# Due times that count each engine's load, and output products that stand behind two units

## The chip, the cores and the metric

The kernel runs on one core of a Trainium2 chip. Its time is the device time of one execution in microseconds; the kernel before takes 1060.63 us (median of 3 runs, 1060.13 to 1060.71). The engines are called as in the profile: PE (matmuls; PEld is its weight load), DVE, ACT and POOL (elementwise engines), and SP, whose queue issues nearly all DMAs.

## The reference

Attention with random features on 8 batches x 8 heads x 576 tokens x 64, and then a gated product on all 4608 tokens:

```python
def phi(x):
    proj = np.einsum('bhsd,md->bhsm', x, omega)
    h = proj - np.sum(x * x, axis=-1, keepdims=True) / 2.0
    h = h - np.max(h, axis=-1, keepdims=True)
    return np.exp(h) / np.sqrt(m)
q_p, k_p = phi(q_s), phi(k_s)
kv = np.einsum('bhsm,bhsd->bhmd', k_p, v);  z = np.sum(k_p, axis=2)
num = np.einsum('bhsm,bhmd->bhsd', q_p, kv)
den = np.einsum('bhsm,bhm->bhs', q_p, z)[..., None] + 1e-06
x = (num / den) ...          # 4608 tokens x 512
a = x @ w_a;  b = x @ w_b    # 512 x 1536 each
return a * b @ w_out         # 1536 x 512
```

## The kernel before

**Numbers.** The second part needs more precision than one pass of PE gives, so each operand is split into a high and a low half and a product is three matmuls (high by high, high by low, low by high).

**Blocks.** The gated product runs in blocks of 512 tokens, b = 0 to 8 (the ninth holds the 64 last tokens of each batch). For b = 0 and 1 (`moe_block`) a step computes `pa` (12 matmuls of 512 columns), `pb` (12), and the four output products `o` of an earlier step (12). From b = 2 on (`moe_block7`) two steps of 128 columns and 512 tokens are computed as a two by two block product with seven instead of eight products. One such run is a **unit** (`unit`): seven products of six matmuls of 256 columns, called A to G here in the order in which they are issued, on two PSUM tiles: A on `p0`, B and C on `p1`, D and E on `p0`, F and G on `p1`. DVE adds (L1253) take them into the sum tile `c`. The add behind C reads both halves of `p1`, and F overwrites a half of it, so F waits for that add. Two units (w = 0 and 1) make one index i; their sums are multiplied (L1303) and split into `ghl` (L333 or L335, and L341), which is what the output products read.

**Output products.** They are collected in the list `left` and issued by `flush` between the products of later units, with a priority number near those units'. For b = 7 and 8 they are a seven product form as well (L1032).

**Attention.** While block b runs on PE, the attention of the next batch is computed pair of heads by pair of heads: `four` (L512: features of keys and queries into the two PSUM tiles `at`), exponentials on ACT, `pkv` (L754), the product `pm` (L822) with rows that went through DRAM, and copies on ACT that free `at` again: `x` from `pm`, `xts` and `k2` from `pkv` (L333). The next `four` needs both `at` tiles, so it waits for the copy `k2`. DVE divides (L773 to L779), ACT scales by it (L783).

**What sets the order.** Nothing of this is issued in the order in which it is written. Each operation is recorded with its engine and an estimated duration, and `plan` then makes a schedule: `schedule` takes, again and again, the operation that can start first on its engine. Where several could start at about the same time, a number decides: on PE and SP the priority `prio`, on DVE, ACT and POOL the due time `due`. Due times come from `dues`, which walks back from the PE's times in the last schedule. `plan` schedules once without due times and three times with them (`ROUNDS`) and keeps the order whose last operation ends first. Each engine then runs its instructions strictly in that order, with semaphores for the dependences.

Of the kernel before, what the change touches and what calls it, by code (L numbers as in the profile page):

```python
# [1 line left out]

# [16 lines left out]
B, H, S, D, M = 8, 8, 576, 64, 128  # L19
# [16 lines left out]
EPS = 1e-6 * M  # L36
KS = NHP

CFG = dict(PORT=0.5, EDF=("DVE", "ACT", "POOL"), ROUNDS=3, SQUEEZE=1, ZS=800, ZB=(1500, 3000, 5000), ZD=(1500, 3000, 4500), HQ=(2500, 4000, 5000), BACK2=(1500, 2500, 4000), TW=(), WAIT=150, RAW=2000, FAST=(0, 1, 2, 3), JOIN0=False, WARM=8, HROOM=["w0", "u1", "w1", "u2", "w2", "u3"], H=3, TURN=(7,), BACK=1500, AT=2, GATES=(-4, -1, 2, 5), SQPE=4, MARGIN=1200, LOAD=2500, SUMS=1000, NATS=(1, 2, 3), CONV=(28000, 2600))

# [14 lines left out]
class Graph:  # L57
# [78 lines left out]
    def dues(self):  # L136

        inf = 1e12
        after = {o: [(n, o) for n in ()] for o in self.ops}
        for o in self.ops:  # L140
            for d in o.deps:
                after[d].append(o)

        last = {}
        for o in self.order:
            for b in o.alloc:
                if b.slot in last:
                    for x in last[b.slot].users:
                        if x is not o:
                            after[x].append(o)  # L150
                last[b.slot] = b
        idle, at, ideal = 0, 0, {}
        for o in self.order:
            if "PE" in o.eng:
                idle += max(0, o.start - at - 5) * CFG["SQUEEZE"]
                at = o.end
                ideal[o] = o.start - idle
        for o in reversed(self.order):
            d = ideal[o] + o.eng["PE"] if o in ideal else inf
            for n in after[o]:  # L160
                same = "PE" in o.eng and "PE" in n.eng
                cost = n.end - n.start if n.bytes else next(iter(n.eng.values()))
                d = min(d, n.due - cost - n.margin - (0 if same else self.LAT + (150 if "PE" in o.eng else 0)))
            o.due = d

    def plan(self):

        self.schedule()
        plans = [(max(o.end for o in self.order), 0, None)]
        for k in range(CFG["ROUNDS"]):  # L170
            self.dues()
# [3 lines left out]
        _, k, due = min(plans, key=lambda p: p[:2])  # L175
        if k < CFG["ROUNDS"]:
            for o in self.ops:
# [4 lines left out]
    def schedule(self, bw=330.0, dma_lat=2000):  # L182
# [29 lines left out]
        while len(done) < len(self.ops):  # L212
            best = None
            for e in engines:
                mine = None
                for o in ready[e]:
# [7 lines left out]
                    else:  # L224


                        wait = CFG["WAIT"] if e == "DVE" and 0 <= o.prio < 4000 else 0
                        pr = o.prio if o.due is None or e not in CFG["EDF"] else o.due
                        key = (max(s - wait, free[e] + 30), pr, o.n)
# [15 lines left out]
            else:  # L245
                o.end = s + o.eng[e]
                if e == "DVE" and o.port:
                    o.end += CFG["PORT"] * max(0, min(o.end, free["POOL"]) - s)
                free[e] = max(s + 30, o.end - self.OVER[e])
# [43 lines left out]
def tile_attention_moe(ctx: ExitStack, tc: tile.TileContext, kqt, kqtt, kqn, kqnt, vx, omst, idn, wab, wout, out):  # L293
    nc = tc.nc
    SQPE = CFG["SQPE"]
# [104 lines left out]
    late = [f"{r}{k}" for k in range(NF - 1, -1, -1) for r in "uw"]  # L400
# [525 lines left out]
    MOE = 10 ** 6  # L926
# [3 lines left out]
    left = []  # L930
# [233 lines left out]

    def flush(seq, n=99):
        for _ in range(min(n, len(left))):
            left.pop(0)(MOE + seq)

# [37 lines left out]
    def moe_block7(b):  # L1208
# [10 lines left out]
        def unit(i, w, C):  # L1219
# [43 lines left out]

            k = 0 if i == NFP - 1 and w else 1
            flush(seq + 3, 5 if i == w == 0 else k)
            product(p0, 1, tcol(tA, 1), (tA, None), scol(0), sr[0], 4)
            if ones7 and w == 0:
# [4 lines left out]

            add(slice(3, 4), p0, slice(1, 2), lambda: c4.ap[:, 1:2], [1], [3])
            flush(seq + 6, k)
            product(p1, 0, tcol(tB, 1), (tB, None), xcol(2, hi_half), xr(2), 7)
            product(p1, 1, lambda k, c: bq.ap[:, k, P * c:P * c + P], (bq, None), scol(3), sr[1], 8)
# [170 lines left out]
```

## Time and profile before

| what | value |
|---|---|
| median of 3 runs | 1060.63 us |
| profiled execution, first to last instruction (span) | 1057.4 us |
| PE busy | 1042.8 us, 7806 matmuls |
| PE weight load busy | 919.1 us |
| DVE busy | 885.7 us |
| ACT busy | 594.5 us |
| POOL busy | 106.0 us |
| granted clock of PE, mean | 0.998 |
| DMA | 314.16 MB, mean 297 GB/s |

The profiled execution is known by its span; the median of the runs is 1060.63 - 1057.4 = 3.2 us more, which is what lies around the first and the last instruction. PE is busy nearly all the time, so its idle stretches and its slow stretches are what an order can change. PE's busy time is modelled from overlapping matmuls; the starts of consecutive matmuls tell more than the sum. A timeline row has the start (us), the length from the first start to the last end, the engine, the line, the names, and in square brackets the idle time before it with what ended it.

### The profile page before, as it was taken

The page shows a single profiled execution, that of the slowest core. Times are in us where ns is not written, and L with a number is a line of the kernel's source. Part 1 is how long each engine was busy: PE and PEld are TensorE (multiplying, and loading weights), DVE is VectorE, ACT ScalarE, POOL GpSimd, SP SyncE. Part 2 cuts the span into 40 slices and gives each one's busy share as a digit, 9 for nine tenths or more (in the row PEclk, how much of TensorE's full clock was granted, in tenths as well). Part 3 has the DMA queues.
Part 4 walks back from the last instruction along what each step waited for, and adds up shares of the span by engine and source line. Part 5 has one row for each costly group of instructions (what it writes and reads, how often), then busy time and mean ns, then how long its engine had stood idle before and what let it go on. Part 6 is the DMA issues. An engine that isn't in the chain of part 4 may idle for free.

```text
span 1057.4 us, 22019 instructions
## 1 busy us (share of the span) xinstructions
PE 1042.8 (99%) x7806; PEld 919.1 (87%) x7806; DVE 885.7 (84%) x2226; ACT 594.5 (56%) x1642; POOL 106.0 (10%) x177
## 2 busy tenths in 40 slices
PE   9999999999999999999999999999999999999998
PEld 7877777877788888888989898989898988999998
DVE  6999999899998688879787788878776677998767
ACT  7897788678765475656455565565464123232211
POOL 0121111111111010201011111111010000000000
PEclk9999999999999999999999999999999999999999
DMA  9777797999899889988989888989888899999991
GB/s 357 274 248 248 239 308 248 315 332 330 280 301 384 279 283 342 312 308 285 326 309 328 295 311 299 341 277 303 270 262 282 274 304 310 325 325 337 354 326 52
DMA packets 123646, 314.16 MB, mean 297 GB/s; under 512 B 17680, under 2 KB 40976, under 8 KB 123536
## 3 DMA queue, kind: packets, MB, share of 16 engines
q1 hardware_dynamic: 122656, 312.10, 86.4%
q8 instruction: 61, 1.00, 0.4%
q10 hardware_dynamic: 880, 0.66, 0.2%
q14 instruction: 49, 0.40, 0.1%
HBM read 255.52 MB, written 57.18 MB: 296 GB/s over the span
## 4 chain that ended last, share of the span: by engine, by line
PE 86%; DVE 8%; ACT 2%; DMA 2%; issue 1%; SPq 0%; DVEq 0%; ACTq 0%
PE p L1243 39%; PE o L962 19%; PE ppk L512 5%; PE o_P L1032 5%; PE pa L1151 4%; PE pb L1151 4%; PE pkv L754 2%; PE pm L822 2%; DVE raw L387 1%; DVE sm L535 1%; PE pn L896 1%; PE p L1032 1%; PE ppq L512 1%; DVE c L1253 1%; PE pkv L884 1%
## 5 line engine op out<-in xcount | busy, mean ns | idle before, releaser
L1253 DVE TENSOR_TENSOR c<-p,c 128x512 f32<-128x512 f32 (+1 forms) x336 | 207.5, 618 | 83.2 <-PE p L1243 79.4
L962 PE MATMUL o<-wo,ghl 128*128 128x512 f32 x1008 | 270.1, 397 | 0.0
L962 PEld LDWEIGHTS o<-wo,ghl 128*128 128x128 f32 x1008 | 176.1, 188 | 31.2 <-DVE ghl L341 0.2
L1243 PE MATMUL p<-Sa,t 128*128 128x256 f32 x1008 | 143.1, 281 | 0.0
L1243 PEld LDWEIGHTS p<-Sa,t 128*128 128x128 f32 x1008 | 131.6, 188 | 4.5
L707 POOL TENSOR_TENSOR z<-hk 128x256 f32<-128x256 f32 x56 | 45.0, 804 | 668.8 <-ACT hk L548 530.9
L783 ACT ACTIVATE hq<-hq,dn 128x128 f32<-128x128 f32 x224 | 70.3, 393 | 33.1 <-DVE dn L779 28.7
L333 ACT COPY c<-p 128x256 f32<-128x256 f32 x84 | 31.1, 370 | 96.5 <-PE p L1243 85.8
L512 PEld LDWEIGHTS ppk<-om,X 64*128 64x128 f32 x504 | 61.3, 188 | 18.6 <-ACT k L333 5.3
L512 PE MATMUL ppk<-om,X 64*128 64x128 f32 x504 | 73.8, 287 | 3.7 <-ACT k L333 3.6
L1151 PE MATMUL pa<-x,wa 128*128 128x512 f32 x288 | 75.0, 403 | 1.0 <-DVE x L341 0.8
L1243 PE MATMUL p<-x,t 128*128 128x256 f32 x504 | 73.9, 282 | 1.5 <-ACT oc L333 1.5
L773 DVE CUSTOM_DVE_ANT_0 zero<-hq,zb 128x128 bf16<-128x128 f32 x224 | 72.1, 322 | 3.9 <-DMA zb<-zdr 1.2
L1243 PEld LDWEIGHTS p<-x,t 128*128 128x128 f32 x504 | 68.8, 188 | 7.0 <-ACT oc L333 1.7
L1243 PE MATMUL p<-Sb,t 128*128 128x256 f32 x504 | 74.3, 283 | 0.0
L1243 PE MATMUL p<-Sb,bq 128*128 128x256 f32 x504 | 73.9, 282 | 0.0
L1151 PE MATMUL pb<-x,wb 128*128 128x512 f32 x288 | 73.7, 399 | 0.0
L512 PE MATMUL ppq<-om,X 64*128 64x128 f32 x504 | 72.9, 286 | 0.1
L548 ACT ACTIVATE hk<-hk,sm 128x128 f32<-128x128 f32 x184 | 59.7, 395 | 16.9 <-DVE sm L542 10.7
L1243 PE MATMUL p<-x,wa 128*128 128x256 f32 x504 | 68.5, 282 | 0.6 <-DVE c L1253 0.6
L1243 PEld LDWEIGHTS p<-x,wa 128*128 128x128 f32 x504 | 65.0, 188 | 4.2 <-DVE c L1253 1.3
L1243 PE MATMUL p<-x,wb 128*128 128x256 f32 x504 | 68.2, 282 | 0.3 <-DVE c L1253 0.2
(194 smaller groups left out, 2026.7 us busy)
## 6 DMA issues: line engine op xcount, KB each, us to landing
t<-td SPq DMA_DIRECT2D x168, 512.0 KB, 5.9
wo<-wod SPq DMA_DIRECT2D x96, 512.0 KB, 5.8
bq<-bd SPq DMA_DIRECT2D x84, 256.0 KB, 6.2
qdr<-qd SPq DMA_DIRECT2D x112, 160.0 KB, 4.4
hq<-qdr SPq DMA_DIRECT2D x28, 640.0 KB, 7.5
X<-in_kqt_dram SPq DMA_DIRECT2D x30, 512.0 KB, 7.1
raw<-in_wab_dram SPq DMA_DIRECT2D x24, 512.0 KB, 7.4
td<-ts SPq DMA_DIRECT2D x24, 512.0 KB, 5.1
```

The source lines that it names most:

```text
L333: nc.scalar.copy(o(), i())
L512: nc.tensor.matmul(pps[w].ap[:, c * M:c * M + M], x()[rows, c * P:c * P + P], om.ap[rows], start=True, stop=True)
L548: g.op({"ACT": 392}, lambda e, c=c, w=w, to=to, at=at: nc.scalar.activation(to.ap[:, at + c], src[w](c), AF.Exp, scale=SC, bias=sm.ap[:, 2 ...
L707: g.op({"POOL": pool2(n)}, lambda e: nc.gpsimd.tensor_tensor(o(), a(), c(), op=ALU.add), r=r, w=w, alloc=list(al), prio=pri, deps=zload[-1 ...
L754: nc.tensor.matmul(pkv.ap[D * j:D * j + D, 0:M], vb.ap[:, vc, 0:D], c(), start=(n == 0), stop=(n == 4))
L773: g.op({"DVE": 413}, lambda e, c=c, j=j, rr=rr, qc=qc: nc.vector.tensor_tensor_reduce(out=junk.ap[rr], in0=qc(), in1=zb.ap[rr, j], scale=1 ...
L783: g.op({"ACT": 392}, lambda e, c=c, src=src: nc.scalar.activation(hq.ap[:, c], src(), AF.Copy, scale=dn.ap[:, c:c + 1]), r=[sd, (dn, None) ...
L962: nc.tensor.matmul(po.ap[:], ghl.ap[:, gi, t * P:(t + 1) * P], wo.ap[:, wi], start=(n == 0 and i == 0), stop=(n == NF - 1 and i == 2))
L1032: nc.tensor.matmul(pb.ap[:, t], A[0](ai)[:, t * P:(t + 1) * P], W[0](wi), start=begin and t == j == 0, stop=stop and t == 1 and j == 2)
L1151: nc.tensor.matmul(pb.ap[:], wt.ap[:, wi, c], xs[c].at(xi), start=(c == 0 and i == 0), stop=(c == NC4 - 1 and i == 2))
L1243: nc.tensor.matmul(pb.ap[:, half], wcol(wi, c), xc(xi, c), start=n == 0, stop=n == 5)
L1253: g.op({"DVE": dve(n)}, lambda e: nc.vector.tensor_tensor(c4.ap[:, o], pb.ap[:, half], y(), op=ALU.add), r=[*((pb, k) for k in range(half. ...
```

## The change

Two things are changed. In `dues`, operations are no longer visited in the reverse of the last schedule's order but by a heap, latest due time first, and for DVE, ACT and POOL (`CAP`) each engine has a pointer: an operation's due time is at most the pointer, and the pointer then moves back by the operation's duration (at least 30 ns). So several operations that would be due at the same moment on one engine get due times one behind the other. And `flush` gives the output products a priority number that is 110 higher. A unit's number is 100 times its index, so an output product now stands behind the rest of the unit in which it is flushed and behind the whole next one.

```diff
-        for o in reversed(self.order):
-            d = ideal[o] + o.eng["PE"] if o in ideal else inf
-            for n in after[o]:
+        before = {o: set() for o in self.ops}
+        left = {o: 0 for o in self.ops}
+        for o in self.ops:
+            for n in set(after[o]):
+                before[n].add(o)
+                left[o] += 1
+        late = {o: ideal[o] + o.eng["PE"] if o in ideal else inf for o in self.ops}
+        ptr = {}
+        heap = [(-late[o], -o.n, o) for o in self.ops if not left[o]]
+        heapq.heapify(heap)
+        while heap:
+            d, _, o = heapq.heappop(heap)
+            e = next(iter(o.eng))
+            cost = o.end - o.start if o.bytes else o.eng[e]
+            if e in CFG["CAP"]:
+                now = min(-d, ptr.get(e, inf))
+                if now < -d:
+                    heapq.heappush(heap, (-now, -o.n, o))
+                    continue
+                ptr[e] = now - max(30, o.eng[e] - self.OVER[e])
+            o.due = -d
+            for n in before[o]:
                 same = "PE" in o.eng and "PE" in n.eng
-                cost = n.end - n.start if n.bytes else next(iter(n.eng.values()))
-                d = min(d, n.due - cost - n.margin - (0 if same else self.LAT + (150 if "PE" in o.eng else 0)))
-            o.due = d
+                late[n] = min(late[n], o.due - cost - o.margin - (0 if same else self.LAT + (150 if "PE" in n.eng else 0)))
+                left[n] -= 1
+                if not left[n]:
+                    heapq.heappush(heap, (-late[n], -n.n, n))
...
     def flush(seq, n=99):
         for _ in range(min(n, len(left))):
-            left.pop(0)(MOE + seq)
+            left.pop(0)(MOE + seq + 110)
```

The instructions on PE are the same 6756 program rows, in another order. On the copies that either ACT or DVE may do, 24 move to DVE (`ghl` and `osb`) and 7 to ACT (weights). Line numbers above 185 are 21 higher in the changed program. Three places show the moves.

**First place:** PE where block 0 ends and block 1 begins, at the attention pair whose product is `pm_1_3`. Before, PE has

```order
L962 MATMUL o0_1_971<-wo11_2192,ghl0_11_2229 128x512 x3
L962 MATMUL o0_2_980<-wo11_2192,ghl0_11_2229 128x512 x3
L962 MATMUL o0_3_990<-wo11_2192,ghl0_11_2229 128x512 x3
L754 MATMUL pkv_2_1_2336<-hk_2_1_2129,v_2_0_1799 64x128 x8
L754 MATMUL pkv_2_1_2336<-htk2_1997,v_2_0_1799 64x128 x2
L822 MATMUL pm_1_3_2338<-hq_1_3_1836,kl7_2328 64x512 x2
L824 MATMUL pkv_2_1_2336<-hq_1_3_1836,kl7_2328 64x64 x2
L512 MATMUL ppk_2_10_2383<-om_67,X_2_1_1934 128x128
```

and now

```order
L983 MATMUL o0_0_1050<-wo10_2025,ghl0_10_2106 128x512 x3
L775 MATMUL pkv_2_1_2287<-hk_2_1_2110,v_2_0_1739 64x128 x8
L775 MATMUL pkv_2_1_2287<-htk2_1940,v_2_0_1739 64x128 x2
L843 MATMUL pm_1_3_2289<-hq_1_3_1771,kl7_2277 64x512 x2
L845 MATMUL pkv_2_1_2287<-hq_1_3_1771,kl7_2277 64x64 x2
L983 MATMUL o0_1_1060<-wo10_2025,ghl0_10_2106 128x512 x3
L983 MATMUL o0_2_1066<-wo10_2025,ghl0_10_2106 128x512 x3
L983 MATMUL o0_3_1076<-wo10_2025,ghl0_10_2106 128x512 x3
L983 MATMUL o0_0_1050<-wo11_2269,ghl0_11_2240 128x512 x3
L533 MATMUL ppk_2_10_2348<-om_67,X_2_1_1886 128x128
```

Before, nothing stood between `pkv`/`pm` and the `four` that needs their PSUM tiles (`ppk_2_10`); now four output products, 12 matmuls, do. On ACT the same place was

```order
L333 COPY kl7_2328<-hq_1_3_1836 128x128
L333 COPY osb0_0_2315<-o0_1_971 128x512
L333 COPY osb0_1_2354<-o0_2_980 128x512
L333 COPY osb0_1_2354<-o0_3_990 128x512
L783 ACTIVATE hq_2_0_2130<-hq_2_0_2130,dn_2_0_2277 128x128
L333 CAST x_1_3_2339<-pm_1_3_2338 128x512
L333 COPY xts1_1481<-pkv_2_1_2336 128x64
L333 COPY k2_2_1_2337<-pkv_2_1_2336 128x128
```

and is now

```order
L354 COPY kl7_2277<-hq_1_3_1771 128x128
L750 COPY zq_2_1_2274<-zq_2_1_2274 32x8 x3
L354 CAST x_1_3_2290<-pm_1_3_2289 128x512
L354 COPY xts1_1497<-pkv_2_1_2287 128x64
L354 COPY k2_2_1_2288<-pkv_2_1_2287 128x128
```

The three copies of the output (`osb`) and one scaling of `hq` no longer stand ahead of the copies that free the PSUM tiles.

**Second place:** ACT in block 0, around `pm_1_0`. Before,

```order
L333 COPY kl4_1426<-hq_1_0_936 128x128
L729 COPY zq_1_2_1423<-zq_1_2_1423 32x8 x3
L497 ACTIVATE natee_1_3_1382<-natee_1_3_1382 128x512
L333 CAST ghl0_5_1459<-a0_5_1358 128x512
L497 ACTIVATE natk_1_3_1398<-natk_1_3_1398 128x512
L383 ACTIVATE raw24_1355<-raw24_1355 128x512
L385 ACTIVATE raw24_1355<-raw24_1355 128x512
L333 CAST x_1_0_1439<-pm_1_0_1438 128x512
L333 COPY xts1_1481<-pkv_1_2_1436 128x64
L333 COPY k2_1_2_1437<-pkv_1_2_1436 128x128
```

and now

```order
L354 COPY kl4_1441<-hq_1_0_944 128x128
L354 CAST wa7_1443<-raw21_1243 128x512
L750 COPY zq_1_2_1437<-zq_1_2_1437 32x8 x3
L404 ACTIVATE raw23_1355<-raw23_1355 128x512
L406 ACTIVATE raw23_1355<-raw23_1355 128x512
L404 ACTIVATE raw24_1369<-raw24_1369 128x512
L354 CAST ghl0_5_1482<-a0_5_1340 128x512
L406 ACTIVATE raw24_1369<-raw24_1369 128x512
L354 CAST x_1_0_1456<-pm_1_0_1455 128x512
L354 COPY xts1_1497<-pkv_1_2_1453 128x64
L354 COPY k2_1_2_1454<-pkv_1_2_1453 128x128
```

The two operations on freshly loaded `nat` tiles went behind; weight conversions (`raw`, `wa7`) came ahead.

**Third place:** PE in a unit of block 6, from C to G. Before,

```order
L1243 MATMUL p1_3757<-Sa_6_0_9640,t6_110_9779 128x256 x3
L1243 MATMUL p1_3757<-Sa_6_1_9653,t6_110_9779 128x256 x3
L962 MATMUL o6_0_9982<-wo6_0_9806,ghl6_0_9960 128x512 x3
L1243 MATMUL p0_3756<-Sa_6_0_9640,t6_110_9779 128x256 x3
L1243 MATMUL p0_3756<-Sa_6_1_9653,t6_110_9779 128x256 x3
L1243 MATMUL p0_3756<-Sb_6_0_9683,t6_111_9886 128x256 x3
L1243 MATMUL p0_3756<-Sb_6_1_9688,t6_111_9886 128x256 x3
L962 MATMUL o6_1_10025<-wo6_0_9806,ghl6_0_9960 128x512 x3
L1243 MATMUL p1_3757<-x_6_2_9118,t6_111_9886 128x256 x3
L1243 MATMUL p1_3757<-x_6_3_9489,t6_111_9886 128x256 x3
```

and now

```order
L1264 MATMUL p1_3741<-Sa_6_0_9626,t6_110_9767 128x256 x3
L1264 MATMUL p1_3741<-Sa_6_1_9639,t6_110_9767 128x256 x3
L1264 MATMUL p0_3740<-Sa_6_0_9626,t6_110_9767 128x256 x3
L1264 MATMUL p0_3740<-Sa_6_1_9639,t6_110_9767 128x256 x3
L1264 MATMUL p0_3740<-Sb_6_0_9666,t6_111_9826 128x256 x3
L1264 MATMUL p0_3740<-Sb_6_1_9672,t6_111_9826 128x256 x3
L1264 MATMUL p1_3741<-x_6_2_9107,t6_111_9826 128x256 x3
L1264 MATMUL p1_3741<-x_6_3_9469,t6_111_9826 128x256 x3
L1264 MATMUL p1_3741<-Sb_6_0_9666,bq6_11_9884 128x256 x3
L1264 MATMUL p1_3741<-Sb_6_1_9672,bq6_11_9884 128x256 x3
L983 MATMUL o6_0_10130<-wo6_1_9905,ghl6_1_9935 128x512 x3
L983 MATMUL o6_1_10138<-wo6_1_9905,ghl6_1_9935 128x512 x3
```

Two output products that stood between C and F are gone from there; all four now follow G. Over the whole program, F comes behind C with only D and E between them in 47 of 84 units, where it was 8.

More of the change, by code (lines that the diff above doesn't have):

```diff
@@ L1 @@
+import heapq
 from contextlib import ExitStack
@@ L37 @@
 KS = NHP
-CFG = dict(PORT=0.5, EDF=("DVE", "ACT", "POOL"), ROUNDS=3, SQUEEZE=1, ZS=800, ZB=(1500, 3000, 5000), ZD=(1500, 3000, 4500), HQ=(2500, 4000, 5000), BACK2=(1500, 2500, 4000), TW=(), WAIT=150, RAW=2000, FAST=(0, 1, 2, 3), JOIN0=False, WARM=8, HROOM=["w0", "u1", "w1", "u2", "w2", "u3"], H=3, TURN=(7,), BACK=1500, AT=2, GATES=(-4, -1, 2, 5), SQPE=4, MARGIN=1200, LOAD=2500, SUMS=1000, NATS=(1, 2, 3), CONV=(28000, 2600))
+CFG = dict(PORT=0.5, EDF=("DVE", "ACT", "POOL"), ROUNDS=3, SQUEEZE=1, CAP=("DVE", "ACT", "POOL"), ZS=800, ZB=(1500, 3000, 5000), ZD=(1500, 3000, 4500), HQ=(2500, 4000, 5000), BACK2=(1500, 2500, 4000), TW=(), WAIT=150, RAW=2000, FAST=(0, 1, 2, 3), JOIN0=False, WARM=8, HROOM=["w0", "u1", "w1", "u2", "w2", "u3"], H=3, TURN=(7,), BACK=1500, AT=2, GATES=(-4, -1, 2, 5), SQPE=4, MARGIN=1200, LOAD=2500, SUMS=1000, NATS=(1, 2, 3), CONV=(28000, 2600))
 class Buf:
```

## The prediction

> **What bounds the kernel now.** I read the page first.
>
> ```profile
> span 1057.4 us, 22019 instructions
> PE 1042.8 (99%) x7806; PEld 919.1 (87%) x7806; DVE 885.7 (84%) x2226; ACT 594.5 (56%) x1642; POOL 106.0 (10%) x177
> PE   9999999999999999999999999999999999999998
> ```
>
> PE is busy in every slice, and the change adds and removes no matmul. So the sum is short: what PE loses by waiting, or by a slow clock, before and after. The profiled execution has 1057.4 us inside its span; the median of the runs, 1060.63, has 3.2 us more, and I carry these 3.2 us along unchanged.
>
> Next the windows, for the stages (length; PE, PEld, DVE, ACT, POOL busy; clock; DMA).
>
> ```profile
> 52.80:105.60 52.80, 51.86 (x309) 40.25 (x308) 51.58 (x125) 44.48 (x113) 11.04 (x14) 1.00 0.79 248
> 105.60:158.40 52.80, 51.31 (x296) 40.10 (x290) 50.78 (x134) 40.57 (x106) 8.14 (x11) 1.00 0.82 273
> 158.40:211.20 52.80, 50.63 (x289) 39.91 (x289) 47.22 (x133) 39.38 (x108) 8.63 (x14) 0.97 0.85 282
> 330.00:590.00 260.00, 260.00 (x2066) 232.49 (x2065) 209.59 (x558) 146.57 (x423) 31.44 (x54) 1.00 0.91 310
> ```
>
> Between 52.8 and 211.2 us PE is idle for 0.94 + 1.49 + 2.17 = 4.6 us, and DVE is nearly full (51.58 and 50.78 of 52.80). From 330 us on PE shows no idle time, and DVE has 50 of 260 us free. So the early stage can gain; the later one can only lose. PE's waits name the causes (total us, times, longest):
>
> ```profile
> PE ppk L512 <- ACT k L333: 3.6, 2, 2.1
> PE pa L1151 <- DVE x L341: 0.8, 2, 0.4
> ```
>
> Two waits of `four` for the copy `k2` are the largest.
>
> **The first place: a wait that goes, and a slow clock behind it.** PE's timeline at the end of block 0:
>
> ```profile
> 182.40 0.28 PE L824 MATMUL pkv<-hq,kl 128*64 128x64 f32 x4
> 184.78 0.48 PE L512 MATMUL ppk<-om,X 64*128 64x128 f32 x2 [2.10 <-ACT k L333]
> 186.95 1.65 PE L1151 MATMUL pa<-x,wa 128*128 128x512 f32 x3
> ```
>
> ACT at the same time:
>
> ```profile
> 181.35 1.55 ACT L333 COPY osb<-o 128x512 f32<-128x512 f32 x3
> 183.58 0.40 ACT L783 ACTIVATE hq<-hq,dn 128x128 f32<-128x128 f32 x1 [0.68 <-DVE dn L779]
> 183.89 0.56 ACT L333 CAST x<-pm 128x512 fp32r<-128x512 f32 x1
> 184.46 0.28 ACT L333 COPY k<-pkv 128x128 f32<-128x128 f32 x1
> ```
>
> Nothing stood on PE between `pkv` and `four`, and on ACT the three `osb` copies and one scaling that itself waited for DVE stood ahead of `x`, `xts` and `k2`. In the new order ACT has only `zq` between `kl7` and `x`. From `x` to the end of `k2` these rows show 183.89 to 184.74, 0.85 us. PE has 12 matmuls of 512 columns in between, which one row of the chain of waits prices:
>
> ```profile
> 249.13 2.77 PE o L962 x12
> ```
>
> 2.77 us of work cover about 1.1 us (the copies and a quarter of a microsecond to start them). The wait of 2.10 us goes; it would come back only if ACT were over 1.6 us late here. Price: -2.10.
>
> The clock fell behind that wait (the column before the last two is the granted share):
>
> ```profile
> 185.00:187.00 2.00, 2.00 (x17) 1.63 (x16) 0.17 (x1) 2.00 (x8) 0.00 (x0) 0.64 0.94 357
> 187.00:189.00 2.00, 2.00 (x6) 1.61 (x6) 1.28 (x2) 1.14 (x3) 0.00 (x0) 0.51 1.04 411
> 189.00:191.00 2.00, 2.00 (x21) 1.47 (x20) 1.37 (x2) 1.39 (x4) 0.00 (x0) 1.00 1.01 357
> ```
>
> It lost 0.36 x 2 + 0.49 x 2 = 1.70 us of PE work. Nowhere else behind the warm-up does a window show that, and the gap of 2.10 us is the longest that PE has; so I take the fall to follow from the gap and to go with it: -1.70 (bounds -1.70 and 0).
>
> The Trainium skill, in "TensorE: Matmul & The Clock Gate", Part 1, says that PE's clock falls to half after an idle window of about 3.4 us, and its closing table allows gaps up to about 3 us. By that rule a gap of 2.10 us would not have done it, the slow stretch would have another cause and stay, and the sum would be 1.7 us smaller. The trace speaks against the rule's length here (half clock right behind 2.10 us), and the measurement decides.
>
> **The second place: part of a wait.** ACT, and PE behind it, around `pm_1_0`:
>
> ```profile
> 104.20 0.29 ACT L333 COPY kl<-hq 128x128 f32<-128x128 f32 x1
> 104.66 0.61 ACT L729 COPY zq<-zq 32x8 f32<-32x8 f32 x3 [0.17 <-DVE zq L724]
> 106.59 0.63 ACT L497 ACTIVATE natee<-natee 128x512 f32<-128x512 f32 x1 [1.32 <-DMA natee<-in_kqnt_dram]
> 107.13 0.60 ACT L333 CAST ghl<-a 128x512 fp32r<-128x512 f32 x1
> 108.72 0.67 ACT L385 ACTIVATE raw<-raw 128x512 int32<-128x512 uint32 x1
> 109.28 0.59 ACT L333 CAST x<-pm 128x512 fp32r<-128x512 f32 x1
> 109.84 0.30 ACT L333 COPY k<-pkv 128x128 f32<-128x128 f32 x1
> ...
> 107.16 1.55 PE L1151 MATMUL pa<-x,wa 128*128 128x512 f32 x6
> 110.20 0.48 PE L512 MATMUL ppk<-om,X 64*128 64x128 f32 x2 [1.49 <-ACT k L333]
> ```
>
> ACT stood 1.32 us for a load, with the copies queued behind it. In the new order that load's operation is behind `k2`. From the end of `kl` (104.49) there now stand `wa7` (0.56, the spacing of such rows: 109.28 - 108.72), `zq` 0.61, four `raw` of 0.56, `ghl` 0.51, and 0.86 from `x` to the end of `k2`: 4.8 us, so `k2` ends at about 109.3 instead of 110.14. PE's cover is 12 matmuls before and after. Price: -0.8 of the 1.49 (bounds -1.49, if `ghl` and `raw` come early, and 0, if one of them waits as `natee` did).
>
> **The start.** In block 0's beginning PE waited 0.8 us for `x_0_2` and `x_0_3` (the second waits row). The new order gives `x_0_2` 5.75 us of matmuls behind its transposes instead of 0.9, counted in the order with the durations above, and `x_0_3` 2.3 instead of 1.5, so both should go; but it gets this by running the last pair of heads earlier, with less work between its own steps. I take 0, with 0.8 either way.
>
> **The later stage: bare products.** Here the change moves most and gains nothing. F needs the DVE add behind C. A bare run in the trace of before (PE, C and D in one row, then F; then the add):
>
> ```profile
> 856.91 1.57 PE L1243 MATMUL p<-Sa,t 128*128 128x256 f32 x12
> 859.03 0.87 PE L1243 MATMUL p<-x,t 128*128 128x256 f32 x6
> ...
> 857.89 0.69 DVE L1253 TENSOR_TENSOR c<-p,c 128x512 f32<-128x512 f32 x1 [2.66 <-PE p L1243]
> ```
>
> A product takes (859.03 - 856.91) / 3 = 0.71 us. C hands over at 857.62, the add starts 0.27 us later and ends at 858.58, 0.45 us before F. Each output product that stood between added 0.69 us to that. So DVE may be about 0.4 us late, no more, at 47 places instead of 8. How late is it? Over the 84 units of before the add starts 0.27 us or little more behind C in most, and more than 0.66 us behind it, where a bare F would wait, in 15; the excess over 0.66 adds up to 4.5 us. The first unit and the last:
>
> ```profile
> 304.73 0.87 PE L1243 MATMUL p<-Sa,t 128*128 128x256 f32 x6
> 305.44 2.92 PE L962 MATMUL o<-wo,ghl 128*128 128x512 f32 x12
> 306.65 0.68 DVE L1253 TENSOR_TENSOR c<-p,c 128x512 f32<-128x512 f32 x1
> ...
> 1040.45 1.57 PE L1243 MATMUL p<-Sa,t 128*128 128x256 f32 x12
> 1041.44 0.69 DVE L1253 TENSOR_TENSOR c<-p,c 128x512 f32<-128x512 f32 x1 [1.91 <-PE p L1243]
> ```
>
> 1.21 us in the first, 0.27 in the last. With the same lateness at random, 47 bare places cost 47 x 4.5 / 84 = 2.5 us. But in the eight bare units of before none was late. In the new order I counted DVE's work between the add behind G and the next add behind C against PE's in the same stretch: it is over 0.39 us too long in one bare unit only (the fourth of block 7, 2.82 against 2.12 us, a wait of 0.3). So 0.3 from one side, 2.5 from the other; I take 1.0, nearer to the count. The next unit's A and B are better off, since four output products now follow G.
>
> The 17 copies more on DVE, 0.69 us each at most by the row of an add of that size, fall where DVE has 50 of 260 us free, so they cost nothing beyond this; without that room they would be up to 12 us of DVE work. DMAs keep number and size; the weights of `o` are held one unit longer, in three buffers, and fetched a unit ahead. At 0.91 busy that is cover enough, and I take 0.
>
> **The sum.** -2.10 - 1.70 - 0.8 + 0 + 1.0 = -3.6: span 1053.8, time 1057.0 us. Its bounds: -2.10 - 1.70 - 1.49 - 0.8 + 0.3 = -5.8, and -2.10 - 1.70 + 0 + 0.8 + 2.5 = -0.5, so 1054.8 to 1060.1. With the clock staying slow by the skill's rule the same sum would be -1.9, 1058.7.
>
> **The rivals.**
>
> A, *slower*: DVE is late at the bare products. The place is F in blocks 2 to 8, the price what the add is late beyond 0.39 us. The fifteen late adds of before were 4.5 / 15 = 0.30 us beyond. If half of the 47 places are like these, they cost 7.1 instead of 1.0, and the time is 1060.6 - 4.6 + 7.1 = 1063.1; if all are, 14.1, and 1070.1; I put it at 1065. For it speaks that an order made with estimated durations leaves a product bare exactly where it thinks DVE just on time; against it, the eight bare units without a wait. It decides for slower from (4.6 + 2.1) / 47 = 0.14 us a place.
>
> B, *no change*: the first 211 us are DVE's, not PE's. DVE was busy 51.58 and 50.78 of 52.80, so PE's saving only brings it sooner to the next wait for DVE. For it: those rows. Against it: both large waits were for ACT's order, and DVE had 5.6 us free where the first stood. Then 4.6 us come back and 1.0 stays: 1060.6 to 1061.6.
>
> C, *much faster*: all idle time between 26 and 330 us goes, since due times that count the load should serve ACT and DVE alike. PE has 4.6 us idle from 52.8 to 211.2 and 1.7 lost to the clock, and 0.8 in the start: -7.1, plus 0.3 for the bare products: 1053.8. Against it: startup and the handing over of `at` still have places with less than 1.5 us of cover, as before.
>
> **How the numbers follow.** The forecast has 0.52, C 0.10, B 0.22, A 0.16. Less than 0.2%, 2.1 us, can't be told from no change in this kernel. Of the forecast's share 0.05 ends above 1058.5, so faster has 0.57, the same 0.27, slower 0.16. The likeliest alone spans 1054.8 to 1060.1; to hold 8 of 10 the range goes down into C and up over B into the lower half of A: 1053 to 1063.
>
> **What would show it.** Right: no row of `ppk` with a wait over 1 us at `pm_1_3`, and a clock of 1.00 there; under 1 us at `pm_1_0`; waits of p L1243 for c L1253 in PE's rows that stay below 2.5 us in all. Wrong: these waits at 5 us or more (A); as much idle time between 52.8 and 330 us as before, but for DVE (B); a half clock without a gap, which would take 1.7 us from the forecast.

## The result and the profile after

The changed kernel takes **1067.34 us** (median of 5 runs, 1064.93 to 1069.06), the kernel before 1060.63 in the same comparison. The ratio is 1.0059, 95% interval 1.0045 to 1.0073: slower by 0.6%, or about 6.7 us of median. The forecast was 1057.0, with a range up to 1063. The profiled execution's span went from 1057.4 to 1065.5 us, so 8.1 us are to be found in the trace. That is 1.4 more than between the medians. In every run on record the time is 1.7 to 1.9 us more than the span of the same run, so the profiled execution of the kernel before took about 1059.2 us and was itself 1.4 us faster than the median. The 3.2 us that the prediction carries along are therefore only some 1.8 us around the span; the rest is the spread from run to run.

The page and PE's waits of the changed kernel (total us, times, longest):

```profile
span 1065.5 us, 22047 instructions
PE 1046.4 (98%) x7806; PEld 923.7 (87%) x7806; DVE 901.1 (85%) x2243; ACT 585.3 (55%) x1625; POOL 114.7 (11%) x177
...
PE p L1264 <- DVE c L1274: 6.0, 6, 2.2
PE p L1053 <- DMA wo<-wod: 1.9, 1, 1.9
PE p L1264 <- DMA bq<-bd: 1.0, 1, 1.0
...
PE ppk L533 <- ACT k L354: 0.6, 1, 0.6
```

The two waits of `four` for `k2` (3.6 us together before) have come down to 0.6 (0.5 more at `ppq`). In their place stand 6.0 us of products that wait for DVE's adds, and a wait for a load of `wo`, the weights of the output products, that the profile of before did not have.

**By stage.** Windows of the changed kernel (length; PE, PEld, DVE, ACT, POOL busy; clock; DMA):

```profile
52.80:105.60 52.80, 51.47 (x309) 40.43 (x310) 51.85 (x130) 49.51 (x126) 13.44 (x17) 1.00 0.76 246
105.60:158.40 52.80, 52.24 (x322) 40.30 (x316) 49.67 (x132) 40.55 (x106) 7.40 (x12) 1.00 0.80 270
158.40:211.20 52.80, 52.40 (x320) 40.54 (x318) 47.75 (x125) 41.10 (x116) 8.69 (x12) 1.00 0.85 281
211.20:330.00 118.80, 117.05 (x757) 95.49 (x756) 112.08 (x288) 80.90 (x220) 19.63 (x26) 1.00 0.92 331
330.00:590.00 260.00, 258.18 (x2045) 230.20 (x2045) 218.78 (x579) 149.05 (x438) 35.88 (x58) 1.00 0.91 310
850.00:1050.00 200.00, 193.24 (x1535) 189.14 (x1535) 159.22 (x321) 52.95 (x122) 0.00 (x0) 0.98 0.84 297
```

and the two of them that the prediction did not show, of the kernel before:

```profile
211.20:330.00 118.80, 118.52 (x775) 95.07 (x774) 111.82 (x290) 86.08 (x236) 16.25 (x24) 1.00 0.93 320
850.00:1050.00 200.00, 197.46 (x1612) 193.15 (x1611) 164.92 (x335) 55.67 (x129) 0.00 (x0) 1.00 0.85 297
```

Length less PE busy is PE's idle time. Before against after it goes 4.60 to 2.29 us between 52.8 and 211.2, 0.28 to 1.75 between 211.2 and 330, 0 to 1.82 between 330 and 590, and 2.54 to 6.76 from 850 to 1050. The clock recovered 1.6 us at 158.4 to 211.2 (it had been 0.97) and lost some 3.4 behind 850. So with the first 52.8 us, which gained 0.5, the early stage gained 4.4, about what was forecast; the middle gave 3.3 back, and the last 200 us cost 7.6. That makes 6.5; the other 1.6 of the 8.1 us are not to be seen in these windows. (Six matmuls of 256 columns are drawn 0.87 us long but follow each other every 0.71 us, so a stall of up to 0.16 us can stay out of the idle time.)

**The predicted places.** PE at `pm_1_3` (178 us) and at `pm_1_0` (108 us) in the changed kernel:

```profile
178.40 3.04 PE L983 MATMUL o<-wo,ghl 128*128 128x512 f32 x12
181.37 0.37 PE L533 MATMUL ppk<-om,X 64*128 64x128 f32 x1
...
108.45 1.57 PE L1172 MATMUL pb<-x,wb 128*128 128x512 f32 x6
109.95 0.48 PE L533 MATMUL ppk<-om,X 64*128 64x128 f32 x2
```

No bracket stands behind either `ppk`: the waits of 2.10 and of 1.49 us are both gone, and so is the half clock behind the first.

**Where it went: block 7.** This is the first block whose output products have the seven-product form. PE at its first output products, then DVE and PE 40 us later:

```profile
882.63 0.87 PE L1053 MATMUL o_P<-wo,ghl 128*128 128x256 f32 x6
885.40 0.95 PE L1053 MATMUL p<-wo,ghl 128*128 128x256 f32 x6 [1.91 <-DMA wo<-wod]
887.03 1.29 PE L1264 MATMUL p<-x,t 128*128 128x256 f32 x6 [0.68 <-ACT oc L354]
```

```profile
927.20 0.69 DVE L999 TENSOR_TENSOR owr<-wo 128x512 f32<-128x512 f32 x1 [2.43 <-DMA wo<-wod]
927.81 0.68 DVE L1274 TENSOR_TENSOR c<-p,c 128x512 f32<-128x512 f32 x1
...
925.50 0.88 PE L1264 MATMUL p<-Sb,bq 128*128 128x256 f32 x6
928.55 1.65 PE L1264 MATMUL p<-x,wa 128*128 128x256 f32 x6 [2.17 <-DVE c L1274]
```

Here it is to be seen who stands behind whom. In block 7 DVE itself reads `wo` (L999: `owr` is the sum of its high and low half, from which the weights of the seven-product form are made). It runs strictly in order. At 924.8 it came to such a sum (of `wo7_6`, by the order), whose load had not landed, and stood 2.43 us; the unit's add, which PE needed before it could overwrite `p`, was queued behind it. So PE's second wait is put down to "DVE c", but it is the same load. A third of this kind follows at 945 us (1.69 us).

The clock fell behind the first two of them:

```profile
886.00:889.00 3.00, 2.33 (x14) 2.12 (x14) 0.00 (x0) 0.59 (x1) 0.00 (x0) 0.74 0.75 286
889.00:892.00 3.00, 3.00 (x20) 3.00 (x20) 2.31 (x6) 1.08 (x3) 0.00 (x0) 0.69 0.77 253
926.00:929.00 3.00, 0.83 (x6) 0.63 (x5) 1.80 (x3) 0.00 (x0) 0.00 (x0) 0.90 1.02 412
929.00:932.00 3.00, 3.00 (x16) 3.00 (x16) 1.85 (x5) 0.37 (x1) 0.00 (x0) 0.53 0.67 268
```

That is 3 x (0.26 + 0.31 + 0.10 + 0.47) = 3.4 us of PE work.

**Why the loads were late.** SP's issues of `wo` and of `xl` (the rows of block 8, read back from DRAM), after and then before:

```profile
850.32 0.38 SPq L365 DMA_DIRECT2D xl<-xtd  x1
852.34 1.64 SPq L365 DMA_DIRECT2D xl<-xtd  x3
854.03 0.55 SPq L365 DMA_DIRECT2D wo<-wod  x1
861.04 0.32 SPq L365 DMA_DIRECT2D wo<-wod  x1
873.83 0.32 SPq L365 DMA_DIRECT2D wo<-wod  x1
880.10 0.32 SPq L365 DMA_DIRECT2D wo<-wod  x1
```

```profile
855.16 0.32 SPq L344 DMA_DIRECT2D xl<-xtd  x1
855.68 1.57 SPq L344 DMA_DIRECT2D wo<-wod  x3
857.30 1.13 SPq L344 DMA_DIRECT2D xl<-xtd  x2
```

By the order of the instructions, the row at 873.83 loads `wo7_1`, the one at 880.10 `wo7_0`, which PE waited for at 883.5 and which landed 5.3 us behind its issue. Before, both were issued by 857.25, 26 us ahead of PE's first use. The order on SP (buffer numbers cut off) shows the reason. Before:

```
xl0<-xtd   wo6_10<-wod10   wo7_1<-wod1   wo7_0<-wod0   xl1<-xtd   xl2<-xtd   ...   wo7_3<-wod3   ...   xl3<-xtd
```

and now:

```
xl0<-xtd   ...   xl1<-xtd   xl2<-xtd   xl3<-xtd   wo6_11<-wod11   ...   wo6_10<-wod10   ...   wo7_1<-wod1   ...   wo7_0<-wod0   ...   wo7_3<-wod3
```

`wo` has three buffers of its own, and in blocks 7 and 8 it may also use two that attention leaves behind, `hk0` and `hq0` (the list `LATE`). `xl` may use these two as well. Buffers of `wo` are given out in the order of the products. With the lag the products of block 6 come later, and so does the load into its last buffer `wo6_10` (issued at 861.04 instead of 855.68); `wo7_1` cannot ask for a buffer before that. The first `xl` comes earlier (850.32 instead of 855.16). So `xl1` and `xl3` take `hk0` and `hq0` first and keep them until the last of block 7's six pairs of loads (in the planner's table of buffers `wo7_1` and `wo7_0` have them before; after, `xl1` and `xl3` have them, and then `wo7_11` and `wo7_10`). So block 7 lost two of its five buffers for five of its six pairs, besides holding each a unit longer.

### The profile page after: what moved, and what is told of

It is laid out like the page before. It is cut to its first block, busy times and chain, and to the rows that moved or that the text cites. A ratio compares the mean times of both kernels' runs of the same rounds, so it can differ in the third digit from the quotient of the medians.

```text
span 1065.5 us, 22047 instructions
## 1 busy us (share of the span) xinstructions
PE 1046.4 (98%) x7806; PEld 923.7 (87%) x7806; DVE 901.1 (85%) x2243; ACT 585.3 (55%) x1625; POOL 114.7 (11%) x177
## 4 chain that ended last, share of the span: by engine, by line
PE 70%; DVE 19%; DMA 6%; ACT 3%; issue 2%; SPq 0%; DVEq 0%; ACTq 0%
PE p L1264 35%; PE o L983 16%; PE ppk L533 5%; PE o_P L1053 3%; PE pkv L775 2%; DVE c L1274 2%; DMA wo<-wod 2%; DVE sm L556 2%; PE pm L843 2%; PE pb L1172 2%; PE pa L1172 2%; DVE zero L794 1%; DVE raw L408 1%; DMA natq<-in_kqn_dram 1%; DVE ghl L362 1%
## 5 line engine op out<-in xcount | busy, mean ns | idle before, releaser
L983 PE MATMUL o<-wo,ghl 128*128 128x512 f32 x1008 | 249.5, 393 | 0.0
L983 PEld LDWEIGHTS o<-wo,ghl 128*128 128x128 f32 x1008 | 183.4, 188 | 36.2
L1264 PE MATMUL p<-Sa,t 128*128 128x256 f32 x1008 | 137.1, 282 | 0.1
L1264 PEld LDWEIGHTS p<-Sa,t 128*128 128x128 f32 x1008 | 125.3, 188 | 2.8 <-ACT c L354 0.3
L1264 PE MATMUL p<-x,wb 128*128 128x256 f32 x504 | 70.9, 284 | 0.8 <-DVE c L1274 0.8
L1264 PEld LDWEIGHTS p<-x,wb 128*128 128x128 f32 x504 | 66.6, 191 | 4.7 <-DVE c L1274 2.1
L569 ACT ACTIVATE hq<-hq,sm 128x128 f32<-128x128 f32 x192 | 66.5, 398 | 6.6 <-DVE sm L564 6.5
```

What stands on the lines that cost most here:

```text
L569: g.op({"ACT": 392}, lambda e, c=c, w=w, to=to, at=at: nc.scalar.activation(to.ap[:, at + c], src[w](c), AF.Exp, scale=SC, bias=sm.ap[:, 2 ...
L983: nc.tensor.matmul(po.ap[:], ghl.ap[:, gi, t * P:(t + 1) * P], wo.ap[:, wi], start=(n == 0 and i == 0), stop=(n == NF - 1 and i == 2))
L1264: nc.tensor.matmul(pb.ap[:, half], wcol(wi, c), xc(xi, c), start=n == 0, stop=n == 5)
```

## The experiments

From the profile came theory **W**: the loss is that of `wo`, late in block 7. Against it stood **D**, that the new due times put DVE's sums of `wo` ahead of the adds, with or without the lag, and **A** of the prediction, DVE late behind bare products in blocks 2 to 6. When W held, it was split: **B3**, the lost buffers alone; **WB**, lost buffers and products that hold them longer; **L**, the lag itself, whatever the buffers. Ratios are to the kernel before, run beside on the same chip (medians 1060.24 to 1060.92 there); each of the other kernels ran 5 to 12 times. "3 at first" means that `hk0` and `hq0` come back to `wo` for the last pair of block 7 (changed, e2), from its fifth pair (e3, e6) or from its fourth (e5).

| run | due times | lag | `wo` buffers in block 7 | median us | ratio, 95% interval |
|---|---|---|---|---|---|
| before | old | 0 | 5 | 1060.63 | 1 |
| changed | new | 110 | 3 at first | 1067.34 | 1.0059 (1.0045 to 1.0073) |
| e1_dues | new | 0 | 5 | 1054.47 | 0.9950 (0.9934 to 0.9965) |
| e2_lag | old | 110 | 3 at first | 1062.33 | 1.0016 (1.0004 to 1.0027) |
| e3_lag_to6 | new | 110 to block 6 | 3 at first | 1056.19 | 0.9965 (0.9953 to 0.9978) |
| e5_landing | new | 110 | 3 at first | 1063.31 | 1.0038 (1.0023 to 1.0053) |
| e6_first_pair | new | 110, but 0 in block 7's first pair | 3 at first | 1062.88 | 1.0029 (1.0014 to 1.0044) |
| e8_dues_wo3 | new | 0 | 3, in block 8 too | 1060.63 | 1.0003 (0.9990 to 1.0017) |
| e9_xl_out | new | 110 | 5 | 1057.80 | 0.9974 (0.9963 to 0.9985) |
| e10_lag_xl_out | old | 110 | 5 | 1056.79 | 0.9971 (0.9960 to 0.9982) |
| e11_xl_out_to6 | new | 110 to block 6 | 5 | 1057.94 | 0.9978 (0.9967 to 0.9989) |
| e12_dues_xl_out | new | 0 | 5 | **1053.64** | 0.9938 (0.9925 to 0.9950) |
| e13_lag10_xl_out | new | 10 | 5 | 1056.06 | 0.9964 (0.9953 to 0.9974) |
| e14_to6_landing | new | 110 to block 6 | 5 | 1056.74 | 0.9965 (0.9953 to 0.9977) |

**The two halves of the change (e1, e2).** The first is the changed kernel without the lag, the second the kernel before with it:

```diff
-            left.pop(0)(MOE + seq + 110)
+            left.pop(0)(MOE + seq)
```

> The new due times alone; the output products have their old priority again. Theory W (in block 7 the products of `o` come later, so the three buffers of `wo` come free later, the loads land late, and PE and DVE stand for them): without the lag nothing of that is left, and the early waits stay away: 1057 to 1060.5. Rival D (the new due times, not the lag, put DVE's sums of `wo` ahead of the unit's adds): the loss of block 7 stays, 1064 to 1068. Rival A of the prediction (DVE late behind bare products in blocks 2 to 6): no bare products here, 1057 to 1060, so this run does not tell A from W.

> The lag alone, on the old due times. Theory W: the loss of block 7 without the gain of the early stage: 1065 to 1070, with waits for wo<-wod behind 880 us on PE or DVE. Rival D: no loss in block 7, 1060 to 1062. Rival A: 1063 to 1070, spread over blocks 2 to 8, and no wait for wo.

Measured 1054.47 and 1062.33. The new due times alone are a gain of 0.5%, more than any theory had; D falls, since no wait for `wo` is left in e1. The lag alone costs 0.16%, less than W had, but with W's waits: 1.8 us of PE for `wo` at 880 us, 2.5 us of DVE. So the halves do not add up: -6.1 and +1.7 would be -4.4, and together they are +6.7.

**Which blocks, and whose estimate (e3, e5).** e3 takes the lag from blocks 7 and 8. e5 keeps it and tells the planner that the loads of `wo` in these blocks land 4.0 us later:

```diff
# e3
+        lag[0] = 0 if seven else 110          # start of moe_block7
-            left.pop(0)(MOE + seq + 110)
+            left.pop(0)(MOE + seq + lag[0])
# e5: Out7.load, and schedule
-                 alloc=[wo], prio=-20, nbytes=P * 2 * E * 4)
+                 alloc=[wo], prio=-20, nbytes=P * 2 * E * 4, lat=4000)
-                o.end = dma_free + dma_lat
+                o.end = dma_free + dma_lat + o.lat
```

> The whole change, but in blocks 7 and 8 (the two with seven output products a pair) the products keep their old priority. Theory W: all of the loss is in those blocks, so 1058 to 1061, level with the kernel before or a little under it. Rival A: blocks 2 to 6 hold 40 of the 47 bare places, so most of the loss stays: 1064 to 1067. Rival D: 1064 to 1068.

> The whole change, but the planner takes the loads of `wo` in blocks 7 and 8 to land 4.0 us later than it did (its own figure is 2.0 us behind the transfer; the trace has 5.4 to 8.7 us from issue to landing). Only the order can change. Theory W: the sums of `wo` no longer stand on DVE ahead of the adds, so the two waits of 2.2 us of PE and the slow clock behind one of them go: 1060 to 1063. If it is the transfers themselves that are late for PE and no order helps (rival T), it stays at 1065 to 1069.

Measured 1056.19 and 1063.31. With the lag in blocks 0 to 6 only, 11 us of the change's time are gone, more than W had. Some 8.7 of them lie behind 850 us, where PE's idle time up to its last matmul fell from 6.76 to 1.47 us and no half clock is left; most of the rest lies early, because the new plan orders the first blocks differently too (up to 211.2 us PE is idle for 1.87 instead of 4.04 us). So most of the loss is in blocks 7 and 8, and A falls as its main cause: 30 bare units are left in blocks 2 to 6, where the changed kernel has 35 (not 40, as the expectation says).

e5 came out 0.3 us above W's range. The better estimate took 4.0 us off by order alone: the two waits behind DVE's sums (2.17 and 1.69 us) shrank to 0.3 each, but PE's wait for `wo7_0` stayed (1.8 us), and one of 2.7 us behind DVE came right after it. That last one is no wait for `wo`. DVE stood twice for a store:

```profile
DVE owr L1000 <- DMA out_dram<-osb: 2.7, 1, 2.7
DVE otf L1004 <- DMA out_dram<-osb: 2.3, 1, 2.3
```

The sums `owr` and `otf` are written into `raw0` and `raw1` (`LATE`), which block 6's output rows `osb` had just used, and the store of these rows had not ended: one more shared buffer. The order cures a sum that stands too early, not a load that is issued too late.

**The first place, and the buffers (e6, e8, e9).** e6 has no lag while block 7 goes through its first pair of units; e8 is e1 with three buffers only; e9 is the whole change, with `xl` sent to other buffers that are free then:

```diff
# e6
+            lag[0] = 0 if b == B - 1 and i == 0 else 110
# e8
-    LATE = dict(wo=["hk0", "hq0"], ...
+    LATE = dict(wo=[], ...
# e9
-   xl = g.buf("xl", [P, SM], F32, f"xl{hp}", ["X0", "X1", "hk0", "hq0", "hq1"])
+   xl = g.buf("xl", [P, SM], F32, f"xl{hp}", ["X0", "X1", "ht2", "v0", "v1"])
```

> The whole change, but while block 7 goes through its first pair of units the products (they are block 6's last) keep their old priority. Theory W, by place: of the 8 us that block 7 loses, the wait for wo7_0 at 883 us and the slow clock behind it go, and the two later waits behind DVE's sums of `wo` stay: 1061 to 1064.5. If it all hangs on that first place (each later wait only a consequence of it): 1058 to 1060.5. If it changes nothing: 1065 to 1069.

> The new due times alone, no lag, but `wo` has its three own buffers only in blocks 7 and 8 (not hk0 and hq0). Theory B3 (the number of buffers alone decides; the lag only lost two of them to block 8's rows `xl`, which now load into hk0 and hq0 first): the loss comes without any lag, 1059 to 1064. Theory WB (it takes both: three buffers and products that hold them a unit longer): 1054 to 1057, as with the lag up to block 6, where three buffers did without a wait.

> The whole change with its lag everywhere; only block 8's rows `xl` may no longer take hk0 and hq0 (they take X0, X1, ht2, v0, v1), so that `wo` has five buffers in block 7, as in the kernel before. Theories B3 and WB: the 8 us of block 7 go, 1057.5 to 1061, no wait for wo<-wod on PE behind 880 us. Rival L (the lag itself, by late products and a DVE that has too much to do behind them, whatever the buffers): 1064 to 1069.

Measured 1062.88, 1060.63 and 1057.80. **e9 settles it.** Its instructions on PE stand word for word as in the changed kernel up to the end of block 6 (5357 of 6756 rows), and nothing but one list of buffers differs, but it is 9.5 us faster. SP and PE in e9, and the window of the last 200 us:

```profile
860.90 1.27 SPq L365 DMA_DIRECT2D wo<-wod  x3
...
883.23 0.87 PE L1053 MATMUL o_P<-wo,ghl 128*128 128x256 f32 x6
884.65 0.86 PE L1053 MATMUL p<-wo,ghl 128*128 128x256 f32 x6
...
850.00:1050.00 200.00, 198.68 (x1612) 195.03 (x1612) 166.43 (x334) 55.50 (x126) 0.00 (x0) 1.00 0.84 297
```

`wo6_10`, `wo7_1` and `wo7_0` are issued in one row, 22 us ahead of their use; the same products run without a wait; idle time is 1.32 instead of 6.76 us and the clock is 1.00. One stand of DVE for `wo` is left (2.13 us up to 868.7), with 0.48 us of PE behind it. L falls.

e8 shows that the lost buffers have their price without any lag too: 1060.63 against 1054.47, 6.2 us, with DVE standing for `wo` four times and PE for DVE eight times between 850 and 970 us:

```profile
DVE owr L999 <- DMA wo<-wod: 3.0, 4, 1.0
...
PE p L1264 <- DVE c L1274: 2.1, 8, 0.4
```

So B3 rather than WB. Two limits: e8 has three buffers in block 8 too, so 6.2 us is the price in both blocks, and up to the last matmul PE stands only 1.8 us more behind 850 than in e1 (4.20 against 2.38); the rest is not in its idle time. e3 and e6 add what the lag does to it: with three buffers at first, but no lag at the passage from block 6, PE did not wait for `wo7_0`. e6 took 4.5 us off, within the range by place, but not in the way expected: the two later waits behind DVE's sums did not stay, others came (1.29 us for `ghl`, 0.71 for `ot`), and its clock fell at 305 us, behind a gap of 1.78 us.

**Was it the buffers, or moving `xl` (e10, e11, e12)?** The edit of e9, on the lag alone, on the lag up to block 6, and on the due times alone:

> The lag alone, on the old due times, with block 8's rows kept out of hk0 and hq0, so that `wo` has five buffers in block 7. The lag alone with the buffers lost took 1062.3, and stood 3 us ahead of the kernel before at the end of block 6. If the buffers are the cause: 1054.5 to 1058. If the old due times have another reason to lose in block 7: 1060 to 1063.

> New due times, the lag up to block 6 only, and the five buffers kept. With the lag up to block 6 and the buffers lost it took 1056.2, with hardly a wait for wo. So the buffers should matter little here: 1054.5 to 1056.5. If it falls below 1054, the lost buffers had a price there too.

> The new due times alone, with block 8's rows kept out of hk0 and hq0. There `wo` had the five buffers already, so this checks that moving `xl` has no price or gain of its own: 1053.5 to 1056. Were it 3 us or more faster than the new due times alone (1054.5), the gain of the run with lag and buffers would be that of moving `xl`, not of the buffers of `wo`.

Measured 1056.79, 1057.94 and 1053.64. Where `wo` had its five buffers already, moving `xl` gained 0.8 us (e12 against e1); where it had lost them, 5.5 (e10 against e2) and 9.5 (e9). e12 is the fastest of all, 0.6% under the kernel before. e11 missed: it was expected at 1054.5 to 1056.5 and came out no faster than e3. Its profile shows a wait of DVE that e3 did not have, and PE behind it:

```profile
866.89 0.69 DVE L1000 TENSOR_TENSOR owr<-wo 128x512 f32<-128x512 f32 x1 [3.23 <-DMA wo<-wod]
...
869.17 0.98 PE L1266 MATMUL p<-x,wb 128*128 128x256 f32 x6 [1.79 <-DVE c L1276]
```

With a buffer free sooner, the planner put the first sum of `wo` 18 us earlier, ahead of three adds, and 6.0 us behind the issue (860.9) the load had only just landed. The planner reckons a load at 330 GB/s and 2.0 us, which for 512 KB is 3.6 us.

**That wait alone (e14).** e11 with the estimate of e5; in its order the sum stands behind the three adds:

> As the run with the lag up to block 6 and the five buffers kept (1057.9), but the planner takes the loads of `wo` in blocks 7 and 8 to land 4.0 us later. In that run DVE stood 3.2 us for the load of wo7_0 at 866.9 us with three adds behind it, PE waited 1.8 us and its clock halved. In the new order the first sum of `wo` stands behind those adds. If the place in DVE's queue is the cause: the wait and the slow clock go (about 3.5 us), 1053.5 to 1055.5. If the load itself holds PE up in any order: 1056.5 to 1059.

Measured 1056.74, 1.2 us less than e11 and above the range expected. In the profiled execution the wait and the half clock are gone (no wait of PE over 0.7 us from 850 to 1050), and its span is 2.8 shorter, 1053.6 against 1056.4. The medians keep less than half of that because the profiled execution of e14 was the fastest of its ten (1055.38, 1.36 below the median), while that of e11 lay 0.24 above its own; what makes the other nine slower no trace shows.

**What is left of the lag's price (e13).** With the buffers kept, the lag still costs 4.2 us on the new due times (e9 against e12). A lag of 10 puts an output product behind its own unit's products only:

```diff
-            left.pop(0)(MOE + seq + 110)
+            left.pop(0)(MOE + seq + 10)
```

> New due times, `wo` with its five buffers (as in the run with the lag of 110, 1057.8, and the one with no lag, 1053.6), and a lag of 10: an output product comes behind the seven products of its own unit only, not of two. The order has as many bare places as with 110 (49 of 84 units have nothing but D and E between C and F). If the bare places cost what is left of the lag's price (theory A, about 2 us of waits for c in blocks 2 to 6, and 2 us elsewhere): 1056 to 1058. If it is that products, and what they hold, are a whole unit older: 1053 to 1055.

Measured 1056.06, which by the time alone would speak for A. The profile says otherwise: e13 has 49 bare units, but from 330 to 590 us, most of blocks 2 to 4, PE did not stand at all, and from 290 to 870 us it waited for `c` twice, 0.8 us:

```profile
330.00:590.00 260.00, 260.00 (x2070) 233.01 (x2069) 212.54 (x568) 153.09 (x444) 34.52 (x59) 1.00 0.91 310
...
PE p L1264 <- DVE c L1274: 0.8, 2, 0.5
```

So bare places cost little as such. What e13 takes more than e12 (2.4 us) lies before 330 us: up to there PE is idle for 7.8 us in e13 and for 5.1 in e12. There the lag moves the output products of blocks 0 and 1 among attention's, and the whole order changes with it; no single wait of it was isolated, so this part of the lag's price stays open. On the old due times the lag with its five buffers even gains (e10, 1056.79 against 1060.46 for the kernel before); why it costs on the new ones is open too.

## Why the prediction was wrong

**What bounds the kernel**: right in the main. PE's idle time and clock account, stage by stage, for 6.5 of the 8.1 us.

**First place** (-2.10, and -1.70 for the clock): right. Between 158.4 and 211.2 us PE's idle time fell from 2.17 to 0.40 and the clock from 0.97 rose to 1.00, 3.4 of the 3.8 us. (The sum's upper end, 1060.1, leaves out the 0 that the text allows for the clock; with it, it would be 1061.8.) **Second place** (-0.8): right in sign, and the whole wait of 1.49 went; another of 0.56 came at 131 us, so the window gained 0.93. **Start** (0, 0.8 either way): it gained 0.5 up to 52.8 us and lost 0.4 up to 105.6. Up to 211 us the sum was -4.6 and the windows show -4.4.

**Bare products** (+1.0, 0.3 to 2.5): right in size, but not the place. PE's waits for `c` in blocks 2 to 6 of the changed kernel, and one for a load in block 2's first unit, are

```profile
306.06 0.97 PE L1264 MATMUL p<-Sb,bq 128*128 128x256 f32 x6 [1.04 <-DMA bq<-bd]
...
395.81 0.98 PE L1264 MATMUL p<-x,t 128*128 128x256 f32 x6 [0.95 <-DVE c L1274]
...
532.91 0.98 PE L1264 MATMUL p<-x,wb 128*128 128x256 f32 x6 [0.78 <-DVE c L1274]
```

One real bare F in block 2 (0.95), and one next unit's A in block 4 (0.78), which the prediction thought better off. The wait for `bq` is a load again, of 256 KB, and was in no term of the sum: with one of 0.70 at 232 us it makes up the 1.5 us that were lost from 211 to 330.

**Copies on DVE** (0): no run tests it alone, and nothing in the runs speaks against it.

**The step that failed** is "the weights of `o` are held one unit longer, in three buffers, and fetched a unit ahead. At 0.91 busy that is cover enough, and I take 0". The term taken as 0 measured 9.5 us (changed kernel against e9). Three things are wrong in it.
- The count. Block 7 had five buffers before, not three; the change took two away. The list that lets `wo` and `xl` share them stands in the program, and the order of the loads on SP showed the swap (all four `xl` ahead of `wo6_11`) before any run.
- The measure of cover. A busy share says nothing of a single load. What counts is the time from the release of a buffer to the load's first use, against the time from issue to landing, which the page of before gave as 5.8 us in the median for `wo`. With the change PE came to `wo7_0` 3.4 us behind its issue (880.10 to 883.5), and the load took 5.3; DVE came to `wo7_6` 6.0 us behind its issue (918.78 to 924.8), and the load took 8.4.
- The queue behind it. Only PE was thought of as a reader of `wo`. In block 7 DVE reads it too, in order, with the unit's adds behind.

**The rivals.** A (slower, 1065) came nearest in time, and for the wrong reason: the waits are indeed written down as "DVE c", but e9 takes away the two large ones (3.1 us in seven waits are left, none over 0.95) with 48 bare units in place. B (the early stage is DVE's, nothing gained) falls: the early gain came, and the due times alone are worth 6.1 us. C (all early idle time gone) was not reached in the changed kernel. With the five buffers the whole change takes 1057.8, close to the 1057.0 of the forecast, though not by the same terms: -5.0 up to 211 us, +3.7 from there to 590, and -1.2 behind 850, where the kernel before had waited 1.5 us for `oc`. These make -2.5, of 3.1 between the medians of that comparison; that the total comes so near the forecast is luck.

## What to carry to other kernels

When a change makes something live longer, list its buffers in each stage, who else may take them, and who would be first in the new order; then compare, load by load, the time from issue to first use with the landing times in the profile, instead of the mean load of the DMA engines. A wait that the profile puts down to an engine may be that of a load: look at what stood ahead of the named instruction in that engine's queue, and at who is queued behind every instruction that reads fresh data. And time the halves of a change apart: here one was worth -0.5% alone, and was hidden by what the other did 700 us later.

## What the runs showed of the hardware

**PE's clock falls when PE idles for about half of a fixed stretch of 3.41 us.** All gaps of PE of 0.9 us and more, from 60 us on, in the fourteen profiled executions (before, changed and the twelve above), with the granted clock of the 4 us behind them:

| gap | times | half clock within the next 4 us |
|---|---|---|
| 0.92 to 1.69 us | 21 | 0 |
| 1.73 to 1.83 us | 7 | 3 (1.78, 1.79, 1.79) |
| 1.91 to 2.69 us | 4 | 4 |

Between 1.73 and 1.83 us the length alone does not decide. The clock records of the traces tell what does. Six of the seven falls last 3.41 us and one 6.83 (e2), and switches lie whole multiples of 3.413 us apart: the two falls of the changed kernel, at 887.46 and 928.42, are 40.96 us apart, 12 times that. So the clock is set at fixed points. Cut at these points, the fourteen traces have 4070 stretches between 60 us and the last matmul. In the seven ahead of a fall PE is idle for 1.78 to 2.61 us; in all others for 1.75 at most. Those next to the limit, and two where a gap is divided:

| run | stretch, us | gap in it | PE idle in it | clock of the next stretch |
|---|---|---|---|---|
| e2 | 879.38 to 882.79 | 1.79 | 1.79 | 0.50 |
| e6 | 301.67 to 305.09 | 1.78 | 1.78 | 0.50 |
| e5 | 881.50 to 884.92 | 1.75 | 1.75 | 1.00 |
| e2 | 179.65 to 183.07 | 1.75 | 1.75 | 1.00 |
| e5 | 301.24 to 304.65 | 1.37 of 1.83 | 1.37 | 1.00 |
| e10 | 178.93 to 182.34 | 1.03 of 1.73 | 1.03 | 1.00 |

A fall costs up to 1.7 us of PE's work (3.41 us at half), in e2 up to 3.4, where PE idled for 0.68 us more in the first slow stretch. Where a gap between some 1.8 and 3.5 us falls among these points thus decides whether it has this price, which fits the spread of one kernel's times: the runs of the kernel before that are listed with the experiments take 1058.3 us in the mean at a mean granted clock of 0.998, 1060.6 at 0.996 and 1063.2 at 0.993.

The Trainium skill, in "TensorE: Matmul & The Clock Gate", Part 1, has the clock fall after at least one idle window of about 3.4 us, and its closing table allows gaps up to about 3 us; no gap here was that long, and seven were followed by a half clock, so the measurement decides. It also says that the window, 3413 ns long, runs freely and does not start with the work; the trace agrees with the length (3.41 us), and gaps of 1.73 and 1.83 us that were divided between two stretches had no half clock behind them.

**A load of 512 KB takes 5 to 8 us to land beside the others.** The profile of before has 5.8 us from issue to landing for `wo` in the median, the two of the changed kernel that were waited for took 5.3 and 8.4, with the DMA engines 0.7 to 1.0 busy around them. The Trainium skill, in "DMA: Bandwidth & Descriptors", "Anatomy of one DMA — SWDGE (gpsimd) path", gives a fixed 2.0 us and the bytes by 436 GB/s for DMAs that GpSimd issues; that would make an estimate of 3.2 us for a load of this size, close to the planner's 3.6. The loads here are issued from SP, so it is not a figure for them, and the trace has more. That the other transfers at the same time are the reason is likely; no run here shows such a load alone.
